# Retention and a SwiGLU layer on Trainium2: the gate and value products of the last two units split once more

## The chip, the cores and the metric

The kernel runs on one core of one Trainium2 chip. All times are device microseconds (us). A core has five engines with queues of their own: TensorE (PE in the profile, with its weight loads shown as PEld), VectorE (DVE), ScalarE (ACT), GpSimd (POOL) and SyncE (SP), which here issues DMA transfers. The metric is the time of one execution, as the median of several runs.

## The reference

The reference is retention over 8 batches, 8 heads, 576 positions and a head size of 64, whose output becomes 4608 tokens of 512 features. These go through an RMS norm and a SwiGLU layer of 1536 hidden features. All of it is float32.

```python
scores = scale * np.matmul(q, k.transpose(0, 1, 3, 2))
ret = scores * Dmat[None, :, :, :]
attn_out = np.matmul(ret, v)
x = attn_out.transpose(0, 2, 1, 3).reshape(B * S, H * D)
rms = np.sqrt(np.mean(x * x, axis=-1, keepdims=True) + 1e-06)
xn = x / rms * rms_g
g = xn @ w_gate
silu = g * (1.0 / (1.0 + np.exp(-g)))
val = xn @ w_val
return silu * val @ w_out
```

## The kernel before

The 4608 tokens are worked in 9 units (u = 0 to 8) of 512. Units 0 and 1 are done early, together with the retention of the first jobs and the making of the weight blocks. Units 2 to 8 run in the loop at the end of the kernel, one after the other. While unit u is in its gate and value products, the retention jobs that make unit u+1's input run between them, as long as there are any (`more`): units 7 and 8 have none beside them.

**Products in fewer multiplications.** A product of two matrices, each cut in 2 by 2 blocks, is made with 7 block products instead of 8: sums and differences of blocks of both operands are formed first, and 7 results are added up into the four blocks of the output. The blocks are called A11, S1, S2, S3, S4, A12, A22. The operand blocks of the weights are made once, early, and lie in DRAM: `w_up_blocks` for gate and value (6 pieces of 1792 KB) and `w_out_blocks` for the output (7 of 1344 KB).

**Gate and value.** `up(u, n)` (line 693) makes one group of a unit, n = 0 to 5; even n is a gate group, odd n the value group of the same hidden features (f = n // 2 * 2). One group is 7 block products (`product`, its matmul is line 702), each of 4 matmuls with 256 moving columns, which show as 8 instructions. The order is A11, S2, S1, A12, S3, S4, A22, with a `yield` after each, so that the loop can put other work at a point (n, i). The PSUM banks x, y, z, w take the products; ACT copies the first (line 728), DVE adds the others from PSUM (`add`, line 709). A finished gate block goes through Silu on ACT (line 723) into `h`; a finished value block is multiplied into `h` by DVE (line 721). After a value group `differences` (line 781) forms two differences of blocks of `h` on DVE. The bank w takes the products S3 and A22, and A22 goes to it after DVE has read S3 out.

**Output.** `across(u)` (line 839) makes the 7 block products of h with the output weights. Here the scheme is used twice, each block product being again 7 products of quarters: 49 of them, each 3 matmuls of 128 columns (line 872). The inner sums of the left side, four tiles i1, i3, i2, i4 for one block product, are made on POOL by `inner_sums(u, n, part)` (lines 817 to 829), into a buffer behind `vi`, or into `sums_x`. Those of the first two products (part 0: what needs the first hidden features alone) are issued at n = 4, i = 1; the rest (part 1) at the start of `across`. The results are kept and added by ACT and DVE (lines 887 and 899) in `vec`, a view of `vi`; then `combine` (line 1061) does 7 additions of 128x4x128 on POOL, and `store(u - 1)` (line 1074) issues 8 DMAs to the output at (n, i) = (1, 4) of the next unit.

**The norm of the next unit.** In group n = 5, ACT squares the four chunks of x of unit u+1 and DVE gathers them (`square`, `gather`, `fold`, `meet`); during `across`, `root`, `scale_x` and `sums_of_x` (line 611) finish the normed x and its block sums `sums_x`.

**The ring.** Weights stream through `ring`, 17408 floats per partition. `pieces` lists them in the order of use, `places` gives each a place, `refill()` (line 652) issues a DMA on SP's queue for every next piece whose place is free, and `used()` (line 682), called after the last product of a piece, frees it and calls `refill()`. One gate or value piece is 3584 floats per partition, one output piece 2688.

**Order.** The final loop stands under a manual schedule: every engine runs its instructions in the order in which the program writes them, and waits on semaphores where an operand or a buffer asks for it. Tile pools: `raw` and `att` (retention), `xp` (x of the units, 3 buffers), `tmp`, and 8 PSUM banks.

Of the kernel before, what the change touches and what calls it, by code (L numbers as in the profile page):

```python
# [10 lines left out]
F32 = mybir.dt.float32  # L11
U32 = mybir.dt.uint32
AF = mybir.ActivationFunctionType
ALU = mybir.AluOpType
P = 128
# [29 lines left out]
def kernel(  # L45
# [11 lines left out]
    nc = tc.nc  # L57
# [3 lines left out]
    NHP = H // 2  # L61
# [19 lines left out]
    raw = ctx.enter_context(tc.tile_pool(name="raw", bufs=1))  # L81
    att = ctx.enter_context(tc.tile_pool(name="att", bufs=2))
    xp = ctx.enter_context(tc.tile_pool(name="xp", bufs=3))
    tmp = ctx.enter_context(tc.tile_pool(name="tmp", bufs=4))
    PS = bass.MemoryType.PSUM
# [9 lines left out]
    def row(name):  # L95
        return tmp.tile([P, U], F32, tag="n", name=name, bufs=3)
# [527 lines left out]

    UP, OUT = 7 * 2 * 2 * P, 7 * NK * P
# [10 lines left out]
    pieces = [("out", 0, n) for n in range(7)] + [("out", 1, n) for n in range(4, 7)]  # L638
    N_FIRST = len(pieces)
    for u in range(2, NU):  # L640
        pieces += [("up", u, n) for n in range(2 * NG)] + [("out", u, n) for n in range(7)]
    places = []
    at = AT_SUMS
    for kind, u, n in pieces:
        size = UP if kind == "up" else OUT
# [24 lines left out]

    def piece(kind, u, n):
        if kind == "out" and u == 1 and n < 4:
            i = pieces.index(("out", 0, n + 3))
        else:
            i = pieces.index((kind, u, n))
        assert i < n_sent and (i == n_used or kind == "out" and u == 0)
        a, z = places[i]
        if kind == "up":
            return ring[:, a:z].rearrange("p (b c f) -> p b c f", b=7, c=2)
        return ring[:, a:z].rearrange("p (c n d) -> p n c d", n=7, c=NK)  # L680

    def used():
        nonlocal n_used
        n_used += 1
        refill()
# [7 lines left out]
    def up(u, n):  # L693


        m, f = n % 2, n // 2 * 2
        w = piece("up", u, n)

        def product(blk, ps, start):
            for i in range(2):  # L700
                for c in range(2):
                    nc.tensor.matmul(  # L702
                        ps[:, i * HU : i * HU + HU], lhsT=w[:, PLACE[blk], c, i * P : i * P + P],
                        rhs=t_of[u][blk][:, c], start=(start and i == c == 0), stop=False,
                        skip_group_check=True,
                    )

        def add(o, a, ps):
            nc.vector.tensor_tensor(out=o, in0=a, in1=pairs_of(ps), op=ALU.add)  # L709

        def result(f, t, nm, a, ps):

            o = h[:, f : f + 2, t * HU : t * HU + HU]
            c = pairs_of(ps)
            if a is not None:
                c = o
                if m:
                    c = pairs_of(temp(f"{nm}_{u}_{n}")) if nm == "c12" else a
                add(c, a, ps)
            if m:  # L720
                nc.vector.tensor_tensor(out=o, in0=o, in1=c, op=ALU.mult)  # L721
# [24 lines left out]
        used()  # L746
        result(f + NH, 0, "c21", u2, w_)
        if m:
            differences(u, f)
        yield  # L750

    def up_plain(u, k, n):
# [28 lines left out]
    def differences(u, f):  # L781

        hh = h_1 if u == 1 else h
        b11, b12, b22 = hh[:, f : f + 2, :HU], hh[:, f : f + 2, HU:], hh[:, NH + f : NH + f + 2, HU:]
        for o, a, b in ((t1_of(u)[:, f : f + 2], b12, b11), (b12, b22, b12)):
            nc.vector.tensor_tensor(out=o, in0=a, in1=b, op=ALU.subtract)
# [52 lines left out]
    def across(u):  # L839
# [148 lines left out]
        for n, nm in enumerate(banks_in_turn):  # L988
# [346 lines left out]

    with tc.manual_schedule():
        start()
        for u in range(2, NU):  # L1340
            j0 = NHP * (u + 1)
            more = u + 1 < B
            for n in range(2 * NG):
                for i, _ in enumerate(up(u, n)):
                    if n == 1 and i == 4:
                        store(u - 1)
                    if n == 2 * NG - 2 and i == 1:
                        inner_sums(u, 0, 0)
                        inner_sums(u, 1, 0)
                    if more and i == 2 and 0 < n <= NHP:  # L1350
                        if j0 + n < len(jobs):
                            prepare(j0 + n)
                            fetch(j0 + n + 1)
                    if u + 1 < NU and n == 2 * NG - 1:
                        if i < NHP:
                            gather(u + 1, i, square(u + 1, i))
                        elif i == NHP:
                            fold(u + 1)
                        elif i == 6:
                            meet(u + 1)  # L1360
                    if (u, n, i) == (2, 2, 1):
                        same_rows()
                    if more and (n, i) == (NHP, 5) and j0 + NHP == len(jobs):
                        values(j0 + NHP - 1)
                if more and n <= NHP and (n or u == 2):
                    if j0 + n < len(jobs):
                        slot(j0 + n, rest=(n > 0))
                    else:
                        carried(j0 + n - 1)
            for i, _ in enumerate(across(u)):  # L1370
# [35 lines left out]
```

## Time and profile before

| what | value |
|---|---|
| runs | 1101.27, 1101.41, 1105.15 us |
| median of these | 1101.41 us |
| the profiled execution, time | 1100.22 us |
| the profiled execution, span | 1098.4 us |
| mean granted TensorE clock | 0.997 |
| PE busy | 1085.5 us |
| DVE, ACT, POOL busy | 727.2, 328.2, 443.8 us |
| moved by DMA | 243.60 MB, mean 222 GB/s |
| unit 7: gate and value, output products | from 883.25 us, from 955.90 us |
| unit 8: gate and value, output products | from 988.82 us, from 1061.3 us |

The span is the time from the first to the last instruction of the profile; the profiled execution's own time is 1.8 us longer. Busy times are sums over the instructions of an engine. In lists of instructions the columns are the start and the length in us, the engine, the line of the kernel, the operation, output and input with their tiles and shapes, how many instructions the row joins, and in brackets the idle time before and what ended it.

### The profile page before, as it was taken

The page shows a single profiled execution, that of the slowest core. Times are in us where ns is not written, and L with a number is a line of the kernel's source. Part 1 is how long each engine was busy: PE and PEld are TensorE (multiplying, and loading weights), DVE is VectorE, ACT ScalarE, POOL GpSimd, SP SyncE. Part 2 cuts the span into 40 slices and gives each one's busy share as a digit, 9 for nine tenths or more (in the row PEclk, how much of TensorE's full clock was granted, in tenths as well). Part 3 has the DMA queues.
Part 4 walks back from the last instruction along what each step waited for, and adds up shares of the span by engine and source line. Part 5 has one row for each costly group of instructions (what it writes and reads, how often), then busy time and mean ns, then how long its engine had stood idle before and what let it go on. Part 6 is the DMA issues. An engine that isn't in the chain of part 4 may idle for free.

```text
span 1098.4 us, 24471 instructions
## 1 busy us (share of the span) xinstructions
PE 1085.5 (99%) x10102; PEld 912.2 (83%) x10102; DVE 727.2 (66%) x1251; ACT 328.2 (30%) x739; POOL 443.8 (40%) x421
## 2 busy tenths in 40 slices
PE   9899999999999999999999999999999999999998
PEld 7744444479988899889988998899888988998898
DVE  3878468877866774677667855677565735674467
ACT  5755564331124412332034203330233111201110
POOL 0026326538430195027702571237321932383236
PEclk9999999999999999999999999999999999999999
DMA  8756787596978876797678865888475755585471
GB/s 210 178 190 235 297 252 214 194 354 176 292 276 226 221 256 225 185 240 241 245 217 200 290 257 148 243 255 291 136 204 198 280 194 174 195 287 160 146 250 42
DMA packets 253871, 243.60 MB, mean 222 GB/s; under 512 B 193216, under 2 KB 213824, under 8 KB 247616
## 3 DMA queue, kind: packets, MB, share of 16 engines
q1 hardware_dynamic: 252320, 241.64, 69.7%
q8 instruction: 79, 1.29, 0.5%
q10 hardware_dynamic: 1440, 0.40, 0.2%
q14 instruction: 32, 0.26, 0.1%
HBM read 211.92 MB, written 30.08 MB: 220 GB/s over the span
## 4 chain that ended last, share of the span: by engine, by line
PE 97%; DVE 1%; issue 1%; ACT 0%; POOL 0%; POOLq 0%; DVEq 0%; ACTq 0%
PE up L762 15%; PE x L702 14%; PE w L702 13%; PE z L702 13%; PE y L702 7%; PE xo L872 6%; PE xp L872 4%; PE zo L872 4%; PE zp L872 3%; PE wo L872 2%; PE yo L872 2%; PE av L382 2%; PE av L402 2%; PE wp L872 2%; PE s L295 2%; PE yp L872 2%
## 5 line engine op out<-in xcount | busy, mean ns | idle before, releaser
L762 PE MATMUL up<-x,ring 128*128 128x512 f32 x384 | 167.1, 594 | 0.0
L702 PE MATMUL x<-x,ring 128*128 128x256 f32 x672 | 161.0, 382 | 0.0
L702 PE MATMUL w<-sums,ring 128*128 128x256 f32 x672 | 158.9, 379 | 0.0
L702 PE MATMUL z<-x,ring 128*128 128x256 f32 x672 | 158.7, 379 | 0.0
L824 POOL TENSOR_TENSOR vi<-h 128x384 f32<-128x384 f32 x32 | 42.4, 1326 | 275.9 <-DVE h L721 266.4
L762 PEld LDWEIGHTS up<-x,ring 128*128 128x128 f32 x384 | 72.2, 190 | 89.3 <-issue 84.7
L702 PEld LDWEIGHTS z<-x,ring 128*128 128x128 f32 x672 | 127.7, 190 | 17.4
L702 PEld LDWEIGHTS w<-sums,ring 128*128 128x128 f32 x672 | 127.6, 190 | 17.4
L702 PEld LDWEIGHTS x<-x,ring 128*128 128x128 f32 x672 | 125.3, 190 | 17.5 <-ACT m L728 0.2
L829 POOL TENSOR_TENSOR vi<-h 128x384 f32<-128x384 f32 (+2 forms) x46 | 43.9, 954 | 149.2 <-DVE h L721 149.2
L1068 POOL TENSOR_TENSOR vi<-vi 128x512 f32<-128x512 f32 (+1 forms) x77 | 78.2, 1028 | 51.9 <-DVE vi L899 35.5
L702 PE MATMUL y<-sums,ring 128*128 128x256 f32 x336 | 79.4, 379 | 0.0
L728 ACT COPY m<-x 128x512 f32<-128x512 f32 x42 | 24.6, 587 | 173.3 <-PE x L702 173.3
L709 DVE TENSOR_TENSOR h<-u,w 128x512 f32<-128x512 f32 x42 | 28.9, 688 | 67.8 <-PE w L702 67.8
L702 PEld LDWEIGHTS y<-sums,ring 128*128 128x128 f32 x336 | 63.8, 190 | 8.7
L709 DVE TENSOR_TENSOR u<-m,y 128x512 f32<-128x512 f32 x42 | 28.8, 686 | 63.2 <-PE y L702 62.5
L723 ACT ACTIVATE h<-h 128x512 f32<-128x512 f32 x63 | 39.7, 629 | 83.3 <-DVE h L709 83.3
L1188 POOL TENSOR_TENSOR vi<-vi 128x512 f32<-128x512 f32 (+1 forms) x24 | 40.7, 1696 | 30.4 <-DVE vi L1177 16.9
L709 DVE TENSOR_TENSOR u<-u,z 128x512 f32<-128x512 f32 x42 | 28.9, 687 | 33.6 <-PE z L702 33.4
L1188 POOL TENSOR_TENSOR ring<-ring 128x512 f32<-128x512 f32 x24 | 30.4, 1273 | 49.6 <-DMA w_up_blocks<-ring 43.9
L426 ACT COPY x<-av 128x192 f32<-128x192 f32 (+6 forms) x136 | 37.8, 278 | 30.0 <-PE av L402 28.5
L829 POOL TENSOR_TENSOR vi<-h,vi 128x384 f32<-128x384 f32 (+2 forms) x46 | 44.5, 968 | 3.6
(327 smaller groups left out, 2039.2 us busy)
## 6 DMA issues: line engine op xcount, KB each, us to landing
ring<-w_out_blocks SPq DMA_DIRECT2D x59, 1344.0 KB, 6.4
ring<-w_up_blocks SPq DMA_DIRECT2D x42, 1792.0 KB, 7.7
w_out_blocks<-vi SPq DMA_DIRECT2D x21, 448.0 KB, 6.2
out_dram<-vi SPq DMA_DIRECT2D x64, 128.0 KB, 3.1
qraw<-in_q_dram SPq DMA_DIRECT2D x96, 72.0 KB, 4.7
kraw<-in_k_dram SPq DMA_DIRECT2D x96, 72.0 KB, 2.7
k<-in_k_dram SPq DMA_DIRECT2D x48, 128.0 KB, 2.8
v<-in_v_dram SPq DMA_DIRECT2D x48, 128.0 KB, 3.1
```

The costliest lines, as they stand in the source:

```text
L295: nc.tensor.matmul(s[e][side(odd), i * L : i * L + L], lhsT=d["kT"][side(e), c * L : c * L + L], rhs=d["qT"][side(e), c * L : c * L + L], ...
L426: nc.scalar.copy(out=o, in_=part)
L702: nc.tensor.matmul(ps[:, i * HU : i * HU + HU], lhsT=w[:, PLACE[blk], c, i * P : i * P + P], rhs=t_of[u][blk][:, c], start=(start and i == ...
L709: nc.vector.tensor_tensor(out=o, in0=a, in1=pairs_of(ps), op=ALU.add)
L723: nc.scalar.activation(out=o, in_=c, func=AF.Silu)
L728: nc.scalar.copy(out=s1, in_=pairs_of(x_))
L762: nc.tensor.matmul(ps, lhsT=w[:, PLACE[blk], c % 2, i * P : i * P + P], rhs=x_of[u][:, c], start=(c == 0), stop=(c == NHP - 1),)
L824: eng.tensor_tensor(out=i1, in0=x12, in1=x11, op=ALU.subtract)
L829: eng.tensor_tensor(out=o[:, c], in0=a[:, c], in1=b[:, c], op=op)
L872: nc.tensor.matmul(ps, lhsT=lhs[:, c], rhs=w[:, s, c], start=((nm, s // 4) not in first), stop=False, skip_group_check=True,)
L1068: eng.tensor_tensor(out=t[:, :, o], in0=t[:, :, x], in1=t[:, :, y], op=ALU.add)
L1188: nc.gpsimd.tensor_tensor(out=t[o], in0=t[x], in1=t[y], op=op)
```

## The change

In units 7 and 8 (`LATE`), the groups n = 1 to 4 (`DEEP`) are made by a new function `up_deep`, where each of the 7 block products is itself made of 7 products of quarters: 49 matmuls of 128x128 by 128 columns in a group, in place of 28 of 256 columns.

- The results of a group stay in a tile `deep_c` of 4 by 7 quarters; `combine_in` adds them up by 7 POOL additions of 128x4x128 at the end of the group (for n = 4 in two times 7 additions of half that size, the first after A12). Silu, the products with the gate and the differences are kept in a list `unfinished` and written later, in the groups that follow (`finish`, `FINISH`).
- The inner sums of x for these groups (`inner_x`, DVE) are made in group n = 0 of units 7 and 8, at i = 0 (4 operations on x) and i = 2 (4 on `sums_x`).
- The inner sums of the weights are made once, on POOL, by `inner_blocks(u, n)` in units 3 to 6 (u = n + 2): 4 operations on six blocks and 4 on the seventh. Seven DMAs on SP's queue (`saves`) put them into a new DRAM tile `w_in_blocks`.
- A deep group's weights come as two "in" pieces of 4096 and 3072 floats per partition. `refill()` issues three DMAs for each: two with parts of `w_up_blocks`, one from `w_in_blocks`.
- The pools `raw` and `att` are closed in unit 7, and the new tiles of `up_deep` take their room.
- Other points: the first inner sums of `across`, in units 3 to 8, go from (4, 1) to (5, 2); in units 7 and 8 `store(u - 1)` goes from (1, 4) to (2, 4); `combine` of units 6 and 7 is written at (1, 0) of the following unit and no longer at the end of `across`.

```diff
+    IN_ORDER = (A11, S1, S2, S3, A12, A22, S4)
+    USED_IN = (A11, S2, S1, S3), (A12, S4, A22)
...
+            elif kind == "in":
+                i, z = HALVES[n[1]]
+                o = o.rearrange("p (b k x) -> p b k x", k=2, x=4 * P)
+                src = w_up_d[n[0]].rearrange("p (b x) -> p b x", b=7)
+                for x, y in spans_of(IN_ORDER[i:z]):
+                    nc.sync.dma_start(
+                        out=o[:, x : x + len(y), 0], in_=src[:, y[0] : y[0] + len(y)]
+                    )
+                src = w_in_d[n[0] - DEEP[0]].rearrange("p (b x) -> p b x", b=7)[:, i:z]
+                o = o[:, :, 1]
...
+    def inner_blocks(u, n):
+        w = piece("up", u, n).rearrange("p b c f -> p b (c f)")
+        d = w_in_d[n - DEEP[0]]
+        t6 = vi[:, NV : NV + 6 * 4 * P].rearrange("p (b s f) -> p b s f", b=6, s=4)
+        t1_ = row(f"inner_{n}").rearrange("p (b s f) -> p b s f", b=1, s=4)
+        for t, b in ((t6, slice(0, 6)), (t1_, slice(6, 7))):
...
+                nc.gpsimd.tensor_tensor(out=o, in0=x, in1=y, op=op)
...
+        saves.extend(lambda i=i: save(i) for i in range(7))
+
+    def inner_x(u, part):
+        if not deep_x1:
+            retention.close()
+            late = ctx.enter_context(tc.tile_pool(name="late", bufs=1))
...
+                nc.vector.tensor_tensor(out=r, in0=a, in1=b, op=op)
+
+    def up_deep(u, n):
...
+            for i, s in enumerate(PARTS):
+                nc.tensor.matmul(
+                    held_in[nm][i // 4][:, i % 4 * P : i % 4 * P + P], lhsT=w[:, IN_AT[s]],
+                    rhs=moving(blk, s), start=(start and i % 4 == 0), stop=False,
+                    skip_group_check=True,
+                )
...
+        product(A11, "x", True)
+        copy(first, "x")
+        yield
+        product(S2, "y", True)
+        add(first, first, "y")
+        if m:
+            finish(len(unfinished) - 4)
+        yield
+        product(S1, "z", True)
+        add(c[:, C22], first, "z")
+        yield
+        product(S3, "w", True)
+        add(c[:, C22], c[:, C22], "w")
+        yield
+        product(A12, "x", False)
+        copy(c[:, C11], "x")
+        if m:
+            finish(len(unfinished))
+        split = n == DEEP[-1] and not m
+        if split:
+            combine_in(slice(0, 2))
+        yield
+        product(S4, "z", False)
+        add(c[:, C12], first, "z")
+        if not m:
+            finish()
+        yield
+        product(A22, "w", False)
+        add(c[:, C21], first, "w")
+        if not m:
+            finish()
+        combine_in(slice(2 * split, 4))
+        ends = [lambda i=i: result(i) for i in range(4)]
+        if m:
+            ends[:2] = [lambda: (result(C11), result(C22))]
+            ends[1:] = [lambda: (result(C12), result(C21)), lambda: differences(u, f)]
+        unfinished.extend(ends)
+        yield
...
-        if u and not last:
+        if u and not last and u + 1 not in LATE:
             combine(slice(0, 4), nc.gpsimd)
...
+    FINISH = {(z + 1, 5): 1, (z + 1, 6): 1, (z + 2, 1): 1} if z % 2 else {(z + 1, 1): 3, (z + 1, 4): 2}
...
-                for i, _ in enumerate(up(u, n)):
-                    if n == 1 and i == 4:
+                deep = u in LATE and n in DEEP
+                if u == n + 2 and n in DEEP:
+                    inner_blocks(u, n)
+                for i, _ in enumerate((up_deep if deep else up)(u, n)):
+                    if saves and (n > NHP - 1 or i % 2) and (u != n + 2 or i > 4):
+                        saves.pop(0)()
+                    if u in LATE and n == 0 and i in (0, 2):
+                        inner_x(u, i // 2)
+                    if u in LATE and (n, i) == (1, 0):
+                        combine(slice(0, 4), nc.gpsimd)
+                    if i == 4 and n == (2 if u in LATE else 1):
                         store(u - 1)
-                    if n == 2 * NG - 2 and i == 1:
+                    if (n, i) == ((2 * NG - 1, 2) if u >= DEEP[0] + 2 else (2 * NG - 2, 1)):
+                        while saves:
+                            saves.pop(0)()
                         inner_sums(u, 0, 0)
                         inner_sums(u, 1, 0)
```

More of the change, by code (lines that the diff above doesn't have):

```diff
@@ L80 @@
     const = ctx.enter_context(tc.tile_pool(name="const", bufs=1))
-    raw = ctx.enter_context(tc.tile_pool(name="raw", bufs=1))
-    att = ctx.enter_context(tc.tile_pool(name="att", bufs=2))
     xp = ctx.enter_context(tc.tile_pool(name="xp", bufs=3))
     tmp = ctx.enter_context(tc.tile_pool(name="tmp", bufs=4))
+    retention = ctx.enter_context(ExitStack())
+    raw = retention.enter_context(tc.tile_pool(name="raw", bufs=1))
+    att = retention.enter_context(tc.tile_pool(name="att", bufs=2))
     PS = bass.MemoryType.PSUM
@@ L623, in sums_of_x, with spans_of @@
         t_of[u] = {A11: b11, A12: b21, S1: b12, A22: t4, S2: t2, S3: t3, S4: b22}
-    UP, OUT = 7 * 2 * 2 * P, 7 * NK * P
+    UP, OUT, IN = 7 * 2 * 2 * P, 7 * NK * P, 7 * P
+    HALVES = (0, 4), (4, 7)
+    DEEP = range(1, 5)
+    LATE = (NU - 2, NU - 1)
+    IN_ORDER = (A11, S1, S2, S3, A12, A22, S4)
+    USED_IN = (A11, S2, S1, S3), (A12, S4, A22)
+    def spans_of(blocks):
+        spans = []
+        for i, b in enumerate(blocks):
+            if spans and spans[-1][1][-1] + 1 == PLACE[b]:
+                spans[-1][1].append(PLACE[b])
+            else:
+                spans.append((i, [PLACE[b]]))
+        return spans
+    assert NHP * (LATE[0] + 1) >= len(jobs)
+    w_in_d = dram.tile([len(DEEP), P, 7 * 4 * P], F32, name="w_in_blocks")
     w_up_d = dram.tile([2 * NG, P, UP], F32, name="w_up_blocks")
@@ L640 @@
     for u in range(2, NU):
-        pieces += [("up", u, n) for n in range(2 * NG)] + [("out", u, n) for n in range(7)]
+        for n in range(2 * NG):
+            if u in LATE and n in DEEP:
+                pieces += [("in", u, (n, i)) for i in range(2)]
+            else:
+                pieces.append(("up", u, n))
+        pieces += [("out", u, n) for n in range(7)]
     places = []
@@ L644 @@
     for kind, u, n in pieces:
-        size = UP if kind == "up" else OUT
+        size = {"up": UP, "out": OUT}.get(kind)
+        if kind == "in":
+            size = (HALVES[n[1]][1] - HALVES[n[1]][0]) * 8 * P
         if at + size > RING:
@@ L679, in piece @@
             return ring[:, a:z].rearrange("p (b c f) -> p b c f", b=7, c=2)
+        if kind == "in":
+            return ring[:, a:z].rearrange("p (b s f) -> p b s f", s=8, f=P)
         return ring[:, a:z].rearrange("p (c n d) -> p n c d", n=7, c=NK)
@@ L749, in up, with save @@
             differences(u, f)
+        yield
+    PARTS = (A12, S4, A22, S3, A11, S2, S1)
+    ENDS = (0, 0), (1, 1), (0, 1), (1, 0)
+    C11, C22, C12, C21 = range(4)
+    deep_c = []
+    deep_x2 = []
+    deep_u = [
+        vi[:, NV + i * IN : NV + i * IN + IN].rearrange("p (s t) -> p s t", s=7) for i in range(2)
+    ]
+    deep_x1 = []
+    unfinished, saves = [], []
+    IN_AT = {A11: 0, A12: 2, A22: 3, S1: 4, S2: 5, S3: 6, S4: 7}
+    def inner_blocks(u, n):
[4 more added lines that the diff above has]
+        for t, b in ((t6, slice(0, 6)), (t1_, slice(6, 7))):
+            a11, a21, a12, a22 = (w[:, b, i * P : i * P + P] for i in range(4))
+            s1, s2, s3, s4 = (t[:, :, i] for i in range(4))
+            for o, x, y, op in (
+                (s3, a11, a21, ALU.subtract), (s1, a21, a22, ALU.add),
+                (s2, s1, a11, ALU.subtract), (s4, a12, s2, ALU.subtract),
+            ):
+                nc.gpsimd.tensor_tensor(out=o, in0=x, in1=y, op=op)
+        def save(i):
+            b = PLACE[IN_ORDER[i]]
+            t = t6[:, b] if b < 6 else t1_[:, 0]
+            nc.sync.dma_start(
+                out=d[:, i * 4 * P : i * 4 * P + 4 * P], in_=t.rearrange("p s f -> p (s f)")
+            )
+        saves.extend(lambda i=i: save(i) for i in range(7))
@@ new lines, in inner_x @@
+    def inner_x(u, part):
+        if not deep_x1:
+            retention.close()
+            late = ctx.enter_context(tc.tile_pool(name="late", bufs=1))
+            deep_c.extend(late.tile([P, 4, 7, P], F32, name=f"deep_c_{i}") for i in range(2))
+            deep_x2.append(late.tile([P, 4, 3, P], F32, name="deep_x2"))
+            deep_x1.append(
+                xp.tile([P, NHP, U], F32, tag="x", name="inner_x")
+                .rearrange("p k (a t h) -> p k a t h", a=2, t=2)
+            )
+        x = x_of[u].rearrange("p (a c) (t s h) -> p c s a t h", c=2, t=2, s=2)
+        y = sums_x.rearrange("p i c (s h) -> p c s i h", s=2)
+        for o, v_ in (((deep_x1[0], x), (deep_x2[0], y))[part],):
+            t1_, t3, t2, t4 = (o[:, i] for i in range(4))
+            x11, x12, x21, x22 = v_[:, 0, 0], v_[:, 0, 1], v_[:, 1, 0], v_[:, 1, 1]
+            for r, a, b, op in (
+                (t1_, x12, x11, ALU.subtract), (t3, x22, x12, ALU.subtract),
+                (t2, t3, x11, ALU.add), (t4, x21, t2, ALU.subtract),
+            ):
+                nc.vector.tensor_tensor(out=r, in0=a, in1=b, op=op)
@@ new lines, in up_deep, with moving, product, halves_of @@
+    def up_deep(u, n):
+        m, f = n % 2, n // 2 * 2
+        c, first = deep_c[n % 2], deep_u[n % 2]
+        held_in = {}
+        def moving(blk, s):
+            x = t_of[u][blk]
+            plain = {A11: (0, 0), A12: (1, 0), S4: (1, 1)}
+            if s in plain:
+                i, t = plain[s]
+                return x[:, i, t * P : t * P + P]
+            kind = {S1: 0, S3: 1, S2: 2, A22: 3}[s]
+            if blk in (S2, S3, A22):
+                return deep_x2[0][:, kind, (S2, S3, A22).index(blk)]
+            return deep_x1[0][:, kind, int(blk in (A12, S4)), int(blk in (S1, S4))]
+        def product(blk, nm, start):
+            half = int(blk in USED_IN[1])
+            w = piece("in", u, (n, half))[:, IN_ORDER.index(blk) - HALVES[half][0]]
+            if start:
+                held_in[nm] = bank(f"{nm}o_{u}_{n}"), bank(f"{nm}p_{u}_{n}")
+            for i, s in enumerate(PARTS):
[3 more added lines that the diff above has]
+                    skip_group_check=True,
+                )
+            if blk == USED_IN[half][-1]:
+                used()
+        def halves_of(t, nm):
+            a, b = held_in[nm]
+            return (
+                (t[:, :4].rearrange("p s t -> p (s t)"), a),
+                (t[:, 4:].rearrange("p s t -> p (s t)"), b[:, : 3 * P]),
+            )
+        def copy(o, nm):
+            for t, ps in halves_of(o, nm):
+                nc.scalar.copy(out=t, in_=ps)
+        def add(o, a, nm):
+            for (t, ps), (x, _) in zip(halves_of(o, nm), halves_of(a, nm)):
+                nc.vector.tensor_tensor(out=t, in0=x, in1=ps, op=ALU.add)
+        def combine_in(which):
+            at = PARTS.index
+            for o, x, y in (
+                (A12, A11, A12), (A11, A11, S2), (S1, A11, S1), (S4, S1, S4), (A11, A11, S3),
+                (S3, S1, S3), (A22, A11, A22),
+            ):
+                nc.gpsimd.tensor_tensor(
+                    out=c[:, which, at(o)], in0=c[:, which, at(x)], in1=c[:, which, at(y)],
+                    op=ALU.add,
+                )
+        def result(i):
+            a, t = ENDS[i]
+            o = h[:, f + a * NH : f + a * NH + 2, t * HU : t * HU + HU]
+            x = c[:, i, :4].rearrange("p s t -> p (s t)").rearrange("p (f t) -> p f t", f=2)
+            if m:
+                nc.vector.tensor_tensor(out=o, in0=o, in1=x, op=ALU.mult)
+            else:
+                nc.scalar.activation(out=o, in_=x, func=AF.Silu)
+        def finish(n_=1):
+            for _ in range(max(0, min(n_, len(unfinished)))):
+                unfinished.pop(0)()
+        product(A11, "x", True)
[31 more added lines that the diff above has]
+        ends = [lambda i=i: result(i) for i in range(4)]
+        if m:
+            ends[:2] = [lambda: (result(C11), result(C22))]
+            ends[1:] = [lambda: (result(C12), result(C21)), lambda: differences(u, f)]
+        unfinished.extend(ends)
@@ L1334, in start @@
             tasks[step[0]](int(step[1:]))
+    z = DEEP[-1]
+    FINISH = {(z + 1, 5): 1, (z + 1, 6): 1, (z + 2, 1): 1} if z % 2 else {(z + 1, 1): 3, (z + 1, 4): 2}
     with tc.manual_schedule():
@@ L1362 @@
                         same_rows()
+                    for _ in range(FINISH.get((n, i), 0) if u in LATE else 0):
+                        unfinished.pop(0)()
                     if more and (n, i) == (NHP, 5) and j0 + NHP == len(jobs):
@@ L1369 @@
                         carried(j0 + n - 1)
+            assert not unfinished and not saves
             for i, _ in enumerate(across(u)):
```

## The prediction

> **What bounds the kernel now.** I read the page first (engines, chain), then the chain of waits by time, then busy time by stretch for unit 7, and last POOL's and DVE's timelines where the change puts work.
>
> ```profile
> span 1098.4 us, 24471 instructions
> PE 1085.5 (99%) x10102; PEld 912.2 (83%) x10102; DVE 727.2 (66%) x1251; ACT 328.2 (30%) x739; POOL 443.8 (40%) x421
> PE 97%; DVE 1%; issue 1%; ACT 0%; POOL 0%; POOLq 0%; DVEq 0%; ACTq 0%
> ```
>
> TensorE is busy for 1085.5 of 1098.4 us and is 97% of the chain. So only two things count: how much PE work there is, and whether PE is ever made to wait. In units 7 and 8 it never waits, as the chain shows:
>
> ```profile
> 914.33 1.73 PE w L702 x8
> ...
> 955.90 1.43 PE xo L872 x12
> ...
> 965.37 1.34 PE xo L872 x12
> ...
> 1086.93 2.21 DVE vi L899 x4
> ```
>
> The columns are start, duration, what. One block product of 256 columns is 8 instructions, 1.73 us (216 ns each). Twelve instructions of 128 columns take 1.34 us (112 ns each). Unit 7 has its groups from 883.25, its output products from 955.9 to 988.8. By stretch (PE, PEld, DVE, ACT, POOL busy, clock, DMA share, GB/s), its groups 0 and 5 and its output products:
>
> ```profile
> 883.20:895.30 12.10, 12.10 (x58) 10.65 (x57) 3.90 (x6) 2.44 (x4) 8.80 (x7) 1.00 0.41 153
> 943.70:955.80 12.10, 12.10 (x59) 10.65 (x58) 7.91 (x12) 3.42 (x6) 4.17 (x5) 1.00 0.66 228
> 955.80:988.80 33.00, 33.00 (x296) 33.00 (x296) 24.96 (x32) 2.91 (x6) 27.73 (x25) 1.00 0.80 282
> ```
>
> PE fills each stretch; POOL is nearly full already in group 0 (8.80 of 12.1, the joins of the unit before) and in the output products (27.73 of 33). What new work there costs is read from these rows:
>
> ```profile
> 868.69 1.48 DVE L621 TENSOR_TENSOR sums<-x 128x512 f32<-128x512 f32 x1
> 871.10 1.33 POOL L829 TENSOR_TENSOR vi<-vi,h 128x384 f32<-128x384 f32 x1
> 884.11 9.11 POOL L1068 TENSOR_TENSOR vi<-vi 128x512 f32<-128x512 f32 x7 [5.02 <-DVE vi L899]
> 891.92 0.69 DVE L709 TENSOR_TENSOR h<-u,w 128x512 f32<-128x512 f32 x1 [2.76 <-PE w L702]
> 908.79 0.69 DVE L786 TENSOR_TENSOR t<-h 128x512 f32<-128x512 f32 x1
> 951.40 1.11 POOL L829 TENSOR_TENSOR vi<-h 128x256 f32<-128x256 f32 x1 [18.03 <-DVE h L721]
> 969.58 1.00 POOL L829 TENSOR_TENSOR vi<-h 128x384 f32<-128x384 f32 x1
> ```
>
> DVE with both inputs in SBUF takes 0.69 us alone (L786) and 1.48 beside a POOL operation (L621); POOL's 384 goes from 1.00 to 1.33. DVE with an input in PSUM keeps 0.69 beside POOL (L709 at 891.92 runs inside the joins). Seven joins take 9.11 us: 1.3 each.
>
> [...]
>
> **PE, the gain.** A deep product is 7 matmuls of 128 columns, 14 instructions by 111.7 ns = 1.564 us, against 1.727: 0.163 us by 7 products, 4 groups, 2 units = 9.2 us less. Bounds: 0 (if such instructions took 123 ns here) to 9.2. I take 9.2, as the 12-instruction row holds all through the output products.
>
> **Costs, each measured on PE's wait; T is a unit's start, T4 and T5 the starts of groups 4 and 5.**
>
> (1) Group 0 of units 7 and 8. The joins of the unit before still run from T+0.86 (884.11 against 883.25): they wait for DVE's add, so their new place in program order moves nothing. Now inner_x puts 4 DVE operations of 512 ahead of DVE's adds (part 0) and 4 of 384 after the second add, both inputs in SBUF. Part 0 beside the joins is an estimated 1.7 each (1.48 was beside POOL's 384; a 512 holds 1.27 rather than 1.00): T+1.25 to T+8. Two adds to T+9.2, part 1 to T+12.9, and the add of bank w, which A22 waits for, is done at T+13.5. PE would start A22 at T+10.36 (893.61 less 883.25). Wait 3.1 us per unit; if DVE ran alone, 0; at most 3.9. I take 3.1, since the joins are surely there: 6.2.
>
> (2) Group 3. The differences of the groups before on DVE meet the 7 joins of group 2 on POOL, and the adds behind them free banks late: 0 to 1.5 per unit, 1.0 taken: 2.0.
>
> (3) Unit 7, group 5. ACT's queue holds two Silu that wait for group 4's joins (about T5+6.8), and behind them the squares of unit 8, on which DVE's gathers and the adds behind these wait: 0 to 3.2, taken 2.5.
>
> (4) Inner sums for the first output product, at the end of units 7 and 8. Before, POOL was idle in groups 1 and 2, did the first parts by 933.4, then waited 18.03 us, and did the rest from 951.40 to 954.4, 4 us early. Now it has 7 joins of group 3 (9.1 us, T4+1.2 to T4+10.3), 14 half joins of group 4 (128x256 at an estimated 0.8 each, 11.2 us, to about T5+10.5), the first parts that were moved to (5,2) (5.1 us by their 927.2 to 933.4 less its contention, to T5+15.6) and then three operations of 0.8: the last is ready at T5+17.7 or more. PE wants it at T5+16.2 in unit 7 (957.84 plus three times 0.67, less 943.68), and about T5+14.8 in unit 8, whose order takes A22 second. Least wait 1.5 + 2.9. In the same 28 us DVE has 11 to 14 operations with two SBUF inputs (4 products of gate and value, differences, gathers); at 0.35 each POOL loses up to 4.5 us. Taken: 4.2 in unit 7, 6.5 in unit 8; at most 7 + 9. Together 10.7, bounds 4.4 to 16.
>
> (5) SP. Each deep group has 6 loads in place of 1, and units 3 to 6 have 7 stores of 256 KB each into w_in_blocks. In unit 6 the last of these stand behind the refills of two pieces (1.38 MB each), and POOL's first inner sums of unit 6, which overwrite that buffer, wait for them:
>
> ```profile
> ring<-w_out_blocks SPq DMA_DIRECT2D x59, 1344.0 KB, 6.4
> ring<-w_up_blocks SPq DMA_DIRECT2D x42, 1792.0 KB, 7.7
> ```
>
> Two such loads behind one another end some 12 us after group 4's end (837.3): stores land at 849 to 850.4, and inner sums of 5 us follow, wanted at 852 to 853: 0 to 6, taken 1.7. The other stores and the later point of store() wait for nothing that PE needs: 0, covered by unit ends 60 us away.
>
> (6) Inner blocks of weights on POOL in units 3 to 5, at 9 to 10 us, in groups where POOL does 0 to 4 us: covered, 0 to 1.5 through DVE, 0.5 taken.
>
> (7) Bytes. A deep group streams 3.67 MB in 10.95 us, 335 GB/s, against 222 on the mean and 282 in the output products; the ring holds about 4 pieces ahead and unit 7's 27.4 MB in some 107 us are 256 GB/s. 0 taken; at 282 GB/s a group would take 13 us, 2.1 over, 16 in all, less what was loaded ahead.
>
> Sum: 6.2 + 2.0 + 2.5 + 10.7 + 1.7 + 0.5 = 23.6 us of waits against 9.2 of gain: +14.4. The profiled run took 1100.22 us (span 1098.4, 1.8 around it), 1.2 under the median of the runs shown: 1100.2 + 14.4 = 1114.6, forecast 1114.
>
> [...]
>
> **Rivals.** A (0.53): the sum, 1106 to 1121. B (0.20), the other side: PE's saving stands and POOL and DVE get through as they do alone, only the least wait of (4) is left: 1100.2 - 9.2 + 4.4 = 1095. For it: POOL idle for 18.03 us before 951.40, 0.69 us on DVE when POOL is quiet. Against: 27.73 of 33 and 8.80 of 12.1 us in just the stretches that get more. It decides once POOL's last inner sum is there by T5+18. C (0.11): half of (1) and (4), losses near the gain: 1100 to 1105. D (0.16): every bound at its top (7.8 + 3 + 3.2 + 16 + 6 + 1.5 = 37.5), or loads that fall behind by (7): 1120 to 1132, middle 1126. That 128-column instructions take 123 ns here, so that nothing is gained, is in D and in A's upper end.
>
> A change under 0.5% (5.5 us) can't be told from none. B's lower half is faster, 0.16; B's rest, C and A's edge are no change, 0.14; slower 0.70. The range 1095 to 1126 leaves out about half of B and half of D, some 0.18.
>
> **What would show it.** PE's block products of groups 1 to 4 at 1.56 us; a gap of PE about T+10 in units 7 and 8 released by DVE's L709-type add; a gap some 15 us after group 5's start, released by POOL's inner sums, larger in unit 8; one about 853 us in unit 6. I am wrong if POOL meets T5+16, if DVE's inner_x takes 0.69 beside the joins, or if gaps are released by DMA.

## The result, and the profile after

The changed kernel takes 1126.72 us (median of 4 runs, 1124.75 to 1130.24) against 1101.34 us before: a ratio of 1.0227, 95% interval 1.0206 to 1.0248. It is slower by 25 us. The forecast was 1114 us and slower; the measured median lies 0.7 us above the end of the range.

The profiled execution of the changed kernel was the slowest of the four, 1130.24 us with a span of 1128.4, so its parts add up to 30.0 us and not to 25. First its page: the span, the engines' busy time, and the chain that ended last, by engine.

```profile
span 1128.4 us, 25505 instructions
PE 1090.0 (97%) x10438; PEld 922.4 (82%) x10438; DVE 771.2 (68%) x1307; ACT 339.0 (30%) x763; POOL 556.0 (49%) x523
PE 85%; POOL 8%; DVE 2%; issue 1%; DMA 1%; SPq 0%; ACT 0%; POOLq 0%; DVEq 0%; ACTq 0%
```

POOL has 112 us more to do (556.0 against 443.8) and is now 8% of the chain, where it was 0%. PE's busy time rose although its work fell, in the main because PE ran at half clock for 23.9 us from 860 us on (granted clock 0.50 from 1020 to 1025 us, for one), and an instruction counts as busy for longer then: a row of twelve that takes 1.50 us at 1099.64 takes 2.77 at 1093.52. What PE waited for from 640 us on (columns: engine, line, what ended the wait; us in total, times, the longest):

```profile
PE xp L1080 <- POOL vi L1037: 8.5, 3, 4.4
PE xo L1080 <- POOL vi L1037: 8.4, 2, 7.4
PE w L740 <- DVE h L747: 5.6, 2, 2.8
PE z L740 <- DVE u L747: 1.0, 2, 0.5
PE w L740 <- DVE u L747: 0.4, 1, 0.4
```

L1037 is `inner_sums` for the output products, L747 the add that reads a bank before the last product of a group goes into it. Before, PE had no wait at all in these units, and no wait here was ended by a DMA. By stretch (PE, PEld, DVE, ACT, POOL busy, granted clock, DMA share, GB/s): group 0, groups 1 to 4, group 5 and output products of unit 7, then group 0, groups 1 to 4 and output products of unit 8, then output products of units 5 and 6:

```profile
893.48:909.43 15.95, 12.62 (x58) 10.48 (x57) 14.16 (x14) 2.41 (x4) 10.53 (x7) 1.00 0.44 149
909.43:953.24 43.81, 43.81 (x393) 43.81 (x392) 29.25 (x46) 10.92 (x21) 28.42 (x23) 1.00 0.91 324
953.24:966.57 13.33, 12.92 (x60) 10.54 (x59) 13.26 (x18) 3.83 (x7) 12.78 (x13) 1.00 0.79 303
966.57:1005.92 39.35, 34.94 (x297) 34.69 (x296) 26.95 (x34) 4.06 (x8) 36.08 (x38) 0.96 0.68 238
...
1005.92:1023.62 17.70, 14.36 (x58) 11.72 (x57) 14.18 (x14) 2.41 (x4) 10.54 (x7) 0.88 0.44 148
1023.62:1068.69 45.07, 45.07 (x393) 45.06 (x392) 29.23 (x46) 11.13 (x21) 28.41 (x23) 0.97 0.82 289
1080.78:1128.40 47.62, 36.09 (x295) 35.52 (x293) 26.32 (x53) 2.75 (x6) 33.89 (x38) 0.89 0.25 81
...
738.58:774.10 35.52, 34.12 (x297) 33.35 (x296) 26.09 (x32) 2.91 (x6) 33.29 (x34) 1.00 0.89 340
855.91:893.48 37.57, 34.84 (x298) 34.64 (x296) 26.13 (x32) 2.91 (x6) 33.84 (x35) 0.95 0.67 229
```

A group before took 12.1 us and the output products 32.9 (37.3 in unit 8, with the end). The gain is there in full: unit 7's four deep groups take 43.81 us, 10.95 each. The losses stand beside it, and two columns tell them apart: PE busy under the stretch's length is waiting, a clock under 1.00 is PE at half clock for a part of the stretch.

What group 0 of unit 7 looks like inside (start and length in us, engine, line, operation):

```profile
894.50 10.85 POOL L1276 TENSOR_TENSOR vi<-vi 128x512 f32<-128x512 f32 x7 [2.62 <-DVE vi L1107]
894.80 3.19 DVE L848 TENSOR_TENSOR inner_x<-x 128x512 f32<-128x512 f32 x2
898.03 1.64 DVE L848 TENSOR_TENSOR inner_x<-inner_x,x 128x512 f32<-128x512 f32 x1
...
906.87 0.68 DVE L747 TENSOR_TENSOR h<-u,w 128x512 f32<-128x512 f32 x1
...
907.60 1.99 PE L740 MATMUL w<-sums,ring 128*128 128x256 f32 x8 [2.82 <-DVE h L747]
```

inner_x takes 1.64 us an operation while the joins run on POOL, the joins take 10.85 us in place of 9.11, and the add of bank w ends at 907.55, 14.1 us after the unit's start; PE's last product waits 2.8 us for it (after 0.5 us at the product before). And at the end of unit 7, with group 5's start at 953.24:

```profile
939.51 27.34 POOL L903 TENSOR_TENSOR deep_c<-deep_c 128x512 f32<-128x512 f32 x24
966.82 1.00 POOL L1032 TENSOR_TENSOR vi<-h 128x384 f32<-128x384 f32 x1
...
973.36 0.72 POOL L1037 TENSOR_TENSOR vi<-h 128x256 f32<-128x256 f32 x1
...
974.13 1.95 PE L1080 MATMUL xp<-ring,vi 128*128 128x128 f32 x10 [4.41 <-POOL vi L1037]
```

POOL adds up deep results without a break until T5 + 13.6 us. The inner sums of the first two output products follow; the second part of i3 of the first is ready at 974.08, T5 + 20.8, and PE, which has waited 4.41 us for it, goes on at once. In unit 8 the first output product waits twice, 0.98 us and then 7.41:

```profile
1092.50 1.23 PE L1080 MATMUL xo<-ring,vi 128*128 128x128 f32 x4 [7.41 <-POOL vi L1037]
```

### The profile page after: what moved, and what is told of

Read it like the earlier page. It is cut to its first block, busy times and chain, and to the rows that moved or that the text cites. A ratio compares the mean times of both kernels' runs of the same rounds, so it can differ in the third digit from the quotient of the medians.

```text
span 1128.4 us, 25505 instructions
## 1 busy us (share of the span) xinstructions
PE 1090.0 (97%) x10438; PEld 922.4 (82%) x10438; DVE 771.2 (68%) x1307; ACT 339.0 (30%) x763; POOL 556.0 (49%) x523
## 4 chain that ended last, share of the span: by engine, by line
PE 85%; POOL 8%; DVE 2%; issue 1%; DMA 1%; SPq 0%; ACT 0%; POOLq 0%; DVEq 0%; ACTq 0%
PE up L970 15%; PE x L740 10%; PE w L740 9%; PE z L740 9%; POOL deep_c L903 6%; PE xo L1080 6%; PE y L740 5%; PE xp L1080 4%; PE zo L1080 4%; PE zp L1080 3%; PE wo L1080 2%; PE yo L1080 2%; PE av L383 2%; PE wp L1080 2%; POOL vi L1037 2%; PE av L403 2%
## 5 line engine op out<-in xcount | busy, mean ns | idle before, releaser
L740 PE MATMUL w<-sums,ring 128*128 128x256 f32 x544 | 130.7, 384 | 6.1 <-DVE h L747 5.6
L740 PE MATMUL x<-x,ring 128*128 128x256 f32 x544 | 131.0, 383 | 1.0 <-issue 1.0
L740 PE MATMUL z<-x,ring 128*128 128x256 f32 x544 | 128.8, 380 | 1.0 <-DVE u L747 1.0
L740 PEld LDWEIGHTS w<-sums,ring 128*128 128x128 f32 x544 | 104.1, 192 | 21.6 <-DVE h L747 6.5
L740 PEld LDWEIGHTS z<-x,ring 128*128 128x128 f32 x544 | 103.1, 190 | 16.1 <-DVE u L747 2.2
L740 PEld LDWEIGHTS x<-x,ring 128*128 128x128 f32 x544 | 100.8, 190 | 15.3 <-issue 1.2
L903 POOL TENSOR_TENSOR deep_c<-deep_c 128x512 f32<-128x512 f32 (+1 forms) x70 | 82.0, 1186 | 43.0 <-DVE deep_c L895 24.0
L1037 POOL TENSOR_TENSOR vi<-vi,h 128x384 f32<-128x384 f32 (+2 forms) x46 | 47.0, 1023 | 62.7 <-DMA w_in_blocks<-vi 59.4
L740 PE MATMUL y<-sums,ring 128*128 128x256 f32 x272 | 64.5, 379 | 0.5 <-issue 0.5
L1037 POOL TENSOR_TENSOR vi<-h 128x384 f32<-128x384 f32 (+2 forms) x46 | 45.7, 993 | 37.1 <-DVE h L759 37.1
L740 PEld LDWEIGHTS y<-sums,ring 128*128 128x128 f32 x272 | 51.6, 190 | 7.9 <-issue 0.9
L747 DVE TENSOR_TENSOR h<-u,w 128x512 f32<-128x512 f32 x34 | 23.4, 688 | 49.9 <-PE w L740 49.9
L747 DVE TENSOR_TENSOR u<-m,y 128x512 f32<-128x512 f32 x34 | 23.3, 686 | 41.5 <-PE y L740 40.8
L1037 POOL TENSOR_TENSOR vi<-h,vi 128x384 f32<-128x384 f32 (+2 forms) x46 | 41.3, 898 | 12.3 <-DMA w_in_blocks<-vi 9.0
```

Of the source, the lines that this page charges most:

```text
L740: nc.tensor.matmul(ps[:, i * HU : i * HU + HU], lhsT=w[:, PLACE[blk], c, i * P : i * P + P], rhs=t_of[u][blk][:, c], start=(start and i == ...
L903: nc.gpsimd.tensor_tensor(out=c[:, which, at(o)], in0=c[:, which, at(x)], in1=c[:, which, at(y)], op=ALU.add,)
L1037: eng.tensor_tensor(out=o[:, c], in0=a[:, c], in1=b[:, c], op=op)
```

## The experiments

The edits are to the changed kernel, one after the other or together. "Before" in the ratios is the kernel before the change, run on the same chip; the experiments themselves ran on several chips. The part of a run ahead of the first output products, where no edit acts, takes 233.6 to 240.0 us in the twelve profiles, with half clock for none to 13.7 us of its first 60 (3.4 in the changed kernel's, and in that before the change). So a difference of 2 or 3 us between medians says little by itself, and the lengths of the stages are the firmer measure.

**1. Joins after inner_x.** One tiny POOL addition that reads the last inner sum of x, ahead of the joins.

```diff
                     if u in LATE and (n, i) == (1, 0):
+                        x_ready = deep_x2[0][:, 3, 2, :1]
+                        nc.gpsimd.tensor_tensor(out=joined, in0=x_ready, in1=x_ready, op=ALU.add)
                         combine(slice(0, 4), nc.gpsimd)
```

> The changed kernel, but the 7 joins of the unit before (combine, POOL) in units 7 and 8 also wait for the last inner sum of x, by one tiny POOL addition ahead of them, so that they run in group 1 and not beside inner_x. Theory (DVE with two SBUF inputs and POOL slow one another in group 0): inner_x takes 0.7 and 0.55 us each, the waits of PE in group 0 of units 7 and 8 (0.5 + 2.8 us each in the profile of the changed kernel) go, and with them the half clock after unit 8's; 7 to 10 us less than the changed kernel, some 1117 to 1120 us. Rival (inner_x is simply too much work ahead of DVE's adds): the waits stay within 1 us of what they are, 1125 to 1127.

Measured: 1120.31 us (1117.96 to 1122.39), 6.4 less than the changed kernel, a little under the 7 to 10 of the theory. By stages the two units' groups are 10.7 us shorter; the part ahead of the first output products is 4.0 us longer in this profile. The timeline of unit 7's group 0 on POOL and DVE, and then group 0 of units 7 and 8 by stretch:

```profile
904.68 9.13 POOL L1277 TENSOR_TENSOR vi<-vi 128x512 f32<-128x512 f32 x7
...
898.86 0.69 DVE L849 TENSOR_TENSOR inner_x<-inner_x,x 128x512 f32<-128x512 f32 x1
```

```profile
896.21:908.30 12.09, 12.09 (x59) 10.64 (x58) 8.46 (x14) 2.44 (x4) 3.61 (x4) 1.00 0.55 197
1004.69:1016.78 12.09, 12.09 (x59) 10.64 (x57) 8.46 (x14) 2.44 (x4) 3.66 (x4) 1.00 0.63 218
```

With the same instructions, an inner sum of x takes 0.69 us and not 1.64, the joins 9.13 and not 10.85, and both groups take 12.09 us with PE busy throughout. It was the meeting of the two engines, not the amount of work. The rival falls.

**2. PE kept busy.** Matmuls whose result nobody reads, where PE would wait for the first inner sums.

```diff
                 lhs = lhs_of[s]
+                if late and n == 0 and u in LATE and s == order[1]:
+                    for _ in range(18 if u == LATE[0] else 32):
+                        nc.tensor.matmul(
+                            vector[nm][1][:, 3 * P :], lhsT=x[:, 0, :P], rhs=w[:, A11, 0],
+                            start=False, stop=False, skip_group_check=True,
+                        )
```

> The changed kernel, with matmuls whose result nobody reads (18 in unit 7, 32 in unit 8, into an unused quarter of a PSUM bank) at the places where PE waits for POOL's inner sums in the first output product. PE is as late as before, but not idle. Theory (the granted clock falls to a half after these waits, and that is a good part of the loss): the half clock near 975 and 1088 us goes, 5 to 7 us less than the changed kernel, 1119 to 1122. Rival (the loss is the wait alone): no difference, 1125 to 1128.

Measured: 1126.85 us, 1122.16 to 1131.8, a range that covers the changed kernel's. The half clock did go at both places (output products of unit 7: clock 1.00 for 0.96; of unit 8: 0.99 for 0.89, and 45.0 us for 47.6), but in the profiled execution it came at one place more, 911 us, behind unit 7's group 0, and stayed twice as long, 6.83 us, behind unit 6's wait; the mean clock of its 1129.9 us was 0.991. So it was run again without those waits, on the kernel of experiment 5:

> The run with joins after inner_x and stores at once, groups 1 to 4 deep (1114.7 us), with the 18 and 32 unread matmuls where PE waits for the inner sums of the first output products. [...] Theory (the half clock after the waits costs what PE runs at half speed: 0.8 us in unit 7 and 2.6 in unit 8, by the stretches of the first run of this kind): 3 to 4 us less, 1110.5 to 1111.7. Rival (the half clock costs half of its 13.7 us or more): 6 us less or more. Rival (no cost): 1114 to 1115.

Measured: 1111.9 us (1110.48 to 1115.83) against 1114.68 (1113.62 to 1115.24). Output products of units 7 and 8, first without and then with the unread matmuls:

```profile
957.03:997.04 40.01, 35.59 (x296) 35.40 (x296) 26.38 (x34) 4.06 (x8) 36.20 (x38) 0.91 0.67 234
1065.05:1112.50 47.45, 36.16 (x295) 35.58 (x293) 26.30 (x53) 2.75 (x6) 33.89 (x38) 0.89 0.24 81
```

```profile
962.09:1000.69 38.60, 38.17 (x332) 37.37 (x332) 27.29 (x34) 4.06 (x8) 36.21 (x38) 1.00 0.69 242
1068.69:1113.50 44.81, 40.40 (x359) 40.02 (x357) 27.44 (x53) 2.75 (x6) 33.87 (x38) 1.00 0.26 86
```

The clock is 1.00 in both stretches, which are 1.4 and 2.6 us shorter though PE has more to do and POOL's 36.2 and 33.9 us are the same. The half clock costs 4.0 us here in the profiled executions and 2.8 between the medians, whose ranges overlap. In unit 8 it costs about a quarter of its 10.2 us: in the changed kernel's profile PE is still waiting for the first 4.8 of them and runs at half speed for 5.4. In unit 7 the half clock lasted 6.8 us in experiment 5 (clock 0.91) and 3.4 in the changed kernel (0.96). For the changed kernel the price there is therefore that of the first run, 0.8 us (38.57 for 39.35).

**3. Groups 1 to 3.** DEEP is 1 to 3, and the first inner sums are back at (4, 1) but in unit 5. In units 7 and 8 this reads parts of h before group 3's last results have been put in, so the output is not the layer's, and the run serves for its waits and its time alone.

```diff
-    DEEP = range(1, 5)
+    DEEP = range(1, 4)
...
-                    if (n, i) == ((2 * NG - 1, 2) if u >= DEEP[0] + 2 else (2 * NG - 2, 1)):
+                    if (n, i) == ((2 * NG - 1, 2) if u == DEEP[-1] + 2 else (2 * NG - 2, 1)):
```

> The changed kernel with groups 1 to 3 deep and group 4 as before, the first inner sums of the output products back at (4, 1) except in unit 5, where stores into w_in_blocks are still under way. Theory (POOL's additions for group 4 make the inner sums late): the waits of 4.4 and 8.4 us at the first output products of units 7 and 8 go, with them their half clocks, and unit 6's stores with their wait; 2.3 us of the gain is given up; group 0's waits and unit 5's stay. 1126.7 less some 20 to 24, plus 2.3: 1105 to 1109. Rival (POOL's group 3 already makes them late): waits of 2 us or more stay in both units, 1112 or above.

Measured: 1112.4 us (1111.76 to 1114.48), 14 less than the changed kernel and not 18 to 22. No wait is left at the output products of units 6, 7 and 8; those of group 0 and unit 5 stay, as both sides said. The time lies in the rival's range, but the rival's waits are not there. The waits named by the theory were right and its sum was too high: beside the waits of 4.4 and 8.4 us and unit 6's 4.6 its 20 to 24 leave 2.5 to 6.5 us for half clock, where experiment 2 gives 3.4, and it took losses of the changed kernel's profiled execution, which is 3.5 us over its median, from that median. Between the two profiled executions the difference is 17.6 us (1130.24 and 1112.67).

**4. Stores at once.** All seven stores go out right behind `inner_blocks`. (The other way, a buffer of its own for six of the seven blocks, 12 KB a partition, does not fit: the pool `att` needs 15.5 KB a partition, and 4.375 are left beside it.)

```diff
                     inner_blocks(u, n)
+                    while saves:
+                        saves.pop(0)()
```

> The changed kernel, with all 7 stores of a group's inner sums of weights issued on SP right behind inner_blocks, ahead of the other loads of that group. In the changed kernel's profile POOL is done with these blocks 27 us or more before the stores go out. Theory (the stores go out late because of their place in SP's queue, and POOL's first inner sums of units 5 and 6 wait for them): unit 5's output products go from 35.5 back to 32.9 us and unit 6's from 37.6 back to 32.9; 6 to 8 us less than the changed kernel, 1119 to 1121. Rival (the bytes collide wherever they stand): output products of units 5 and 6 stay above 35 us, or PE waits for the ring's loads elsewhere.

Measured: 1124.84 us, 1120.84 to 1127.79: 2 us less, not 6 to 8, with ranges that overlap. Output products of units 5 and 6 (first two rows) and group 0 of units 7 and 8, then what PE waited for from 640 to 900 us:

```profile
740.68:773.59 32.91, 32.91 (x298) 32.91 (x296) 24.97 (x33) 2.91 (x6) 27.78 (x25) 1.00 0.86 321
855.42:888.34 32.92, 32.92 (x298) 32.92 (x297) 24.98 (x33) 2.91 (x6) 27.78 (x25) 1.00 0.74 260
888.34:905.85 17.51, 14.18 (x59) 11.53 (x57) 14.17 (x14) 2.41 (x4) 10.53 (x7) 0.91 0.40 136
1002.33:1018.29 15.96, 12.62 (x58) 10.48 (x57) 14.17 (x14) 2.41 (x4) 10.54 (x7) 1.00 0.47 164
```

```profile
PE w L740 <- DVE h L747: 2.9, 1, 2.9
PE av L403 <- ACT tick L392: 0.6, 1, 0.6
PE z L740 <- DVE u L747: 0.5, 1, 0.5
```

Both output products are back at 32.9 us, so the late stores were what held POOL up there. But unit 5's groups now take 86.5 us for 82.5, with a new wait of 2.9 us, on DVE (the last row of the waits is unit 7's group 0). DVE is late there because its transpose of the next q waits 5.1 us, and q's load stands behind the seven stores in SP's queue: issued from 712.54 on, where the stores begin at 703.05. The rival is half right: the stores do collide, by their place in the queue, with loads that are not the ring's.

The last two rows of the fence show the clock once more. Group 0's waits are the same in both units, yet the half clock came in unit 7 here (clock 0.91, unit 8's 1.00) and in unit 8 in the changed kernel's profile (0.88, unit 7's 1.00).

**5. Joins and stores together**, experiments 1 and 4.

> The stores at once, and the joins after inner_x: both edits in the changed kernel, with groups 1 to 4 deep. What is left is then the late inner sums at the first output products of units 7 and 8 and their half clock. Theory (the losses add up): 1126.7 less 6.4 (joins after inner_x) less some 7 (stores): 1112 to 1115, with waits of PE of 4.4 and 8.4 us left. Rival (POOL's chain is late because everything ahead of it is, so that its waits change too): waits that differ by over 2 us, and a time outside 1110 to 1117.

Measured: 1114.68 us (1113.62 to 1115.24). PE's waits from 740 us on:

```profile
PE xo L1081 <- POOL vi L1038: 8.4, 2, 7.4
PE xp L1081 <- POOL vi L1038: 4.4, 1, 4.4
PE w L741 <- DVE u L748: 0.4, 1, 0.4
```

The waits at the first output products are what they were, to 0.1 us, without those ahead of them: the losses add up, and POOL's lateness there comes neither from group 0 nor from the stores. Its runs lie within 1.6 us, where the changed kernel's spread over 5.5.

**6. Groups 1 to 3, and 1 and 2, with both edits.** The first inner sums are where all they read has been written.

```diff
-    DEEP = range(1, 5)
+    DEEP = range(1, 4)
...
+                    if (n, i) == ((2 * NG - 1, 2) if u == DEEP[-1] + 2 or u in LATE else (2 * NG - 2, 1)):
```

> Joins after inner_x, stores at once, groups 1 to 3 deep, and in units 7 and 8 the first inner sums at (5, 2), where all they read has been written. Theory: no PE wait over 1 us is left in units 7 and 8, a deep group takes 10.95 us against 12.09, so 6 by 1.14 = 6.9 us less than before, less some 2 to 3 us for unit 3's and 4's inner blocks and the last group: 1096 to 1098, faster than both. Rival (POOL is still late, with the first inner sums only at (5, 2)): waits of 2 us or more at the first output products, 1102 or above.

> As the run before with groups 1 and 2 deep alone, and all first inner sums at (4, 1) as in the kernel before. Theory: 4 by 1.14 = 4.6 us less than before, less 1 to 2.5: 1098 to 1100, slower than with groups 1 to 3. Rival (with group 3 POOL is late): faster than with groups 1 to 3.

Measured: 1100.81 us with three groups (ratio 1.0001, 0.9989 to 1.0012) and 1100.3 with two (0.9986, 0.9975 to 0.9998). With three groups that is 3 to 5 us over what was expected: no wait is left in units 7 and 8, but unit 5's groups take 86.8 us for 82.5, by the stores' place (a wait of 2.4 us on DVE, and half clock behind it: 0.98 on the mean of the stretch). With two groups, which have no stores in unit 5, it is 0.3 us over the expected 1098 to 1100; two and three are level.

**7. Stores spread.** Three groups as in experiment 6, but the stores not at once: they stand behind their own group's loads and ahead of the next group's.

```diff
-                    if saves and (n > NHP - 1 or i % 2) and (u != n + 2 or i > 4):
+                    for _ in range(min(len(saves), (i > 2) if u == n + 2 else 2 * (i < 2))):
                         saves.pop(0)()
```

> Groups 1 to 3 deep, joins after inner_x, and the stores of the weights' inner sums behind the loads for the retention of their own group (i = 3 to 6) and ahead of the next group's (i = 0 and 1), where the run with stores at once had them ahead of the loads and DVE's transposes 4 us late in unit 5. Theory: unit 5's groups go from 86.8 back to some 82.5 us and its output products stay at 32.9; 4 us less than that run (1100.8): 1096 to 1098, faster than the kernel before by 0.3 to 0.5%. Rival (seven stores cost the loads their place wherever they stand): unit 5 stays 3 us or more over the kernel before, 1099 or above.

Measured: 1097.9 us (1096.45 to 1098.45), ratio 0.9966, interval 0.9953 to 0.998: faster than both kernels. Groups 1 to 3 of units 7 and 8, then unit 5's groups and output products:

```profile
900.44:933.32 32.88, 32.88 (x296) 32.88 (x294) 23.24 (x36) 6.80 (x13) 23.23 (x19) 1.00 0.86 294
1002.63:1035.51 32.88, 32.88 (x295) 32.87 (x294) 23.24 (x36) 6.80 (x13) 23.18 (x19) 1.00 0.86 288
658.18:740.72 82.54, 82.54 (x900) 72.47 (x899) 51.31 (x98) 29.15 (x74) 27.24 (x28) 1.00 0.77 216
740.72:773.63 32.91, 32.91 (x297) 32.91 (x296) 24.94 (x33) 2.91 (x6) 27.73 (x25) 1.00 0.90 347
```

A deep group takes 10.96 us, PE is busy throughout, and unit 5 is as before the change. Of the 7 us gained about half is still lost in unit 3's groups (85.7 us for 82.5), in a wait of 1.0 us for a DVE add and one of 1.7 in the middle of a product, for which the profile names no releaser. What makes that one stays open.

**8. Four groups, with the first product's inner sums on DVE**, in units 7 and 8, on experiment 7's kernel. Unit 6, which has stores again with group 4, issues two of them at each point of that group.

```diff
-                        inner_sums(u, 0, 0)
+                        inner_sums(u, 0, 0, nc.vector if u in LATE else nc.gpsimd)
...
         result(f + NH, 0, "c21", u2, w_)
+        if u in LATE and n == 2 * NG - 1:
+            inner_sums(u, 0, 1, nc.vector)
```

> The run with stores spread (1097.9 us), with group 4 deep again, and in units 7 and 8 the inner sums of the first output product on DVE in place of POOL: 4 operations at (5, 2), 3 behind the last value block. POOL keeps those of the second product. Theory (POOL's queue alone made the first product late: its joins ended at T5 + 13.6 us, and the first product's 2.6 + 2.4 us stood behind them): the first product's waits of 4.4 and 8.4 us shrink to 2 us or less each, 2.3 us are gained by group 4: 1096 to 1100. [...]

Measured: 1105.44 us (ratio 1.0039, 1.0025 to 1.0053). PE's waits from 850 us on:

```profile
PE w L741 <- DVE u L748: 4.3, 2, 3.1
PE xo L1083 <- DVE vi L1040: 1.7, 1, 1.7
PE xp L1083 <- DVE vi L1040: 0.9, 2, 0.7
PE ms L567 <- DVE fold L557: 0.2, 1, 0.2
```

The first products' waits fall from 4.4 and 8.4 us to 0.9 and 1.7, but group 5 now waits 4.3 us for DVE's adds. The theory is half right: POOL's queue made the products late, but DVE has no room in group 5 to take the work over, and the time lies 5.4 us over the theory's range. Four groups stay 7.5 us behind three.

## Why the prediction was right and wrong

The side, the places and most of the mechanism were right, but for unit 5 and the clock; the sum was 16 us too small against the profiled execution (11 against the medians). By its own terms, against the stage lengths of the two profiles:

| term | forecast | profile | what it was |
|---|---|---|---|
| gain of the deep groups | -9.2 | -9.2 | 10.95 us a group in unit 7 |
| (1) group 0, units 7 and 8 | 6.2 | 10.7 | waits of 3.3 each; the rest mostly half clock, 1.3 of it in unit 8's group 1 |
| (2) group 3's adds | 2.0 | 0 | no wait |
| (3) unit 7's group 5 | 2.5 | 1.2 | one wait of 0.4 in PE's records |
| (4) first output products | 10.7 | 16.8 | waits of 4.4 and 8.4; the rest mostly half clock |
| (5) stores of inner sums | 1.7 | 7.2 | 2.6 in unit 5 (a wait of 1.4); 4.6 in unit 6 (a wait of 2.7, the rest mostly half clock) |
| (6) inner blocks, units 3 and 4 | 0.5 | 2.0 | 1.5 in two waits without a named releaser |
| start, before the change acts | 0 | 1.2 | |

The gain, and the 1.564 us of a deep product behind it, held to 0.1 us.

Term (1) was right in mechanism and size where it spoke of waits: 3.1 us forecast, 3.3 measured, an estimated 1.7 us per inner sum and 1.64 in the trace. Experiment 1 shows it, by taking the meeting away and leaving the work. Beside the joins DVE's first four operations came about 1.64 us apart, less than the 1.96 that 0.69 and a join's 1.27, one after the other, would make.

Term (4) was right in its chain and nearly in its waits (4.2 and 6.5 forecast, 4.4 and 8.4 measured). It had the joins of group 4 end at T5 + 10.5 us; they ended at T5 + 13.6. The 14 half joins took 1.00 us each on the mean where it had 0.8: four in unit 7 took 0.72 to 0.73 us and the other ten 1.05 to 1.23. So the 3.1 us are close to the 2.7 that the prediction added apart for DVE's operations beside them. Experiment 8 shows that POOL's queue was the cause.

The first step that failed is "The other stores and the later point of store() wait for nothing that PE needs: 0". Unit 5 has the same wait as unit 6: the stores come out late by their place in SP's queue, behind loads for retention in unit 5 and refills of the ring in unit 6, and POOL's inner sums overwrite the buffer that the stores read. First unit 5, then unit 6:

```profile
734.73 1.06 SPq L821 DMA_DIRECT2D w_in_blocks<-vi  x2
...
737.33 0.46 POOL L1037 TENSOR_TENSOR vi<-vi,h 128x128 f32<-128x128 f32 x1 [13.93 <-DMA w_in_blocks<-vi]
...
844.66 2.87 SPq L821 DMA_DIRECT2D w_in_blocks<-vi  x5
...
856.42 0.46 POOL L1037 TENSOR_TENSOR vi<-vi,h 128x128 f32<-128x128 f32 x1 [19.42 <-DMA w_in_blocks<-vi]
```

Finished blocks stood for long: in unit 6 POOL was done with them at 798.6 us, and the stores were issued from 828 to 848. For unit 6 the prediction had this path and priced it at 1.7 us in 0 to 6; the wait was 2.7, and the rest of the 4.6 is mostly half clock. For unit 5 it had nothing, and 2.6 us were lost. Experiment 4 shows the cause, since both output products come back to 32.9 us.

The second is the larger: the sum held nothing for the granted clock. In the changed kernel's profile PE ran at half clock four times from 860 us on. Experiment 1 gives its price in unit 8's groups 0 to 4: 62.8 us against 55.9, of which 3.3 are waits and 3.5 half clock. Experiment 2 gives 0.8 and 2.6 us at the output products of units 7 and 8. Unit 6's was not tried by itself; the stretch there leaves 1.9 us beside its wait. Together that is some 8.8 us of the 16 that were missing. Half clock came not only at the waits of (4), of 4.4 and 7.4 us, but also after a wait of 2.7 us (unit 6) and in the last of two waits of 0.5 and 2.8 us with a product between them (unit 8's group 0).

Terms (2) and (3) were too high, by 3.3 us together. The rival of loads that fall behind did not happen: the deep groups of unit 7 drew 324 GB/s, and no wait of PE there was ended by a DMA. Term (7) counted 27.4 MB for unit 7 where its pieces make 28.0, which changes nothing in it.

## What to carry to other kernels

When work is taken from the engine that bounds a kernel by giving more to others, cost the others' queues at the stage's narrowest point, not over the span: here POOL was 49% busy and still 8% of the chain. Two engines that slowed each other (DVE's inner sums from 0.69 to 1.64 us each, POOL's seven joins from 9.13 to 10.85) were kept apart here by one false dependency, which won back 6.4 us without removing any work. A transfer that frees a buffer must be placed in its queue by who waits for that buffer, and by who waits for the transfers behind it.

## What the runs showed that was not expected

From 860 us on, the half clock of the changed kernel's profile lasted 3.41 us twice, 6.83 and 10.24 us: one, two and three times the same length. It came at waits that sum to 3.3 us with matmuls between them, and at the same waits it sometimes did not come: it came in unit 8's group 0 alone in the changed kernel's profile (clock 0.88, unit 7's 1.00), and in unit 7's alone in experiment 4's (0.91, unit 8's 1.00). Whether that is why the changed kernel's runs spread over 5.5 us is not shown: those of experiment 5, with fewer waits, spread over 1.6, but those of experiment 2's second run, with fewer still, over 5.4.
